# Two divisions and the stores of their rows, moved three slots later on GpSimd and SyncE

## The chip, the core and the metric

The kernel runs on one core of a Trainium2 chip. The core has a matrix engine (TensorE, PE in the profile, with its weight loads as PEld), a vector engine (VectorE, DVE), an activation engine (ScalarE, ACT), a general engine (GpSimd, POOL) and SyncE (SP), which here only issues transfers. Each engine works through its own list of instructions in order, and an instruction that waits holds up all that stand behind it on that engine. Transfers between memory (HBM) and the on-chip buffers go through 16 DMA engines. They are issued either by SyncE (the hardware queue q1) or by GpSimd (the software queue q0). The metric is the time of one execution in device microseconds, as a median of runs.

## The reference

What is computed is a linear attention followed by a two-layer network. With `phi(x) = [exp(p), exp(-p)]`, where `p = x @ w_phi` less the largest absolute value of its row:

```
q_p, k_p = phi(q), phi(k)                 # 8 batches x 8 heads x 576 rows, 64 -> 2 x 128 features
kv  = k_p^T @ v;   z = sum of k_p over rows
x   = (q_p @ kv) / (q_p . z + 1e-6)       # 4608 tokens x 512
h   = x @ w_in                            # 512 -> 2048
g   = max(h, 0) + alpha * min(h, 0)
out = g @ w_out                           # 2048 -> 512
```

## The kernel before, in words

The attention goes through 32 pairs of heads, one after the other, interleaved in a software pipeline. For pair `i` the numerator (128 rows of two heads by 576 tokens) is copied to a tile `s`, and the denominators are inverted by DVE, written to a small array `rec_d` in memory, and read back spread over the partitions into a tile `rr` (`spread`, line 533, two transfers). GpSimd then multiplies `rr = s * rr` (`finish`, line 538), which is the division of the reference, and SyncE writes the tile to `x_d` in memory (`store`, line 541).

Behind the attention comes the network. Its first block of 512 tokens is computed plainly: for each of 16 slices of the hidden layer PE computes `h` (`up2`, lines 584 to 586), ACT and DVE make `r`, `g`, `gh` and `gl` of it (lines 261, 265, 142, 152), and PE adds the slice to four output banks (`down2`, lines 594 to 596). The weights of this block are loaded by SyncE (`load_up` 663, `load_down` 651) as buffers come free. The other eight blocks go two at a time through a scheme with seven products instead of eight, which needs sums and differences of weight blocks. These sums are made once, beside the first block, by `sums` (line 697): GpSimd loads four blocks of a weight (`su<-a_d` or `sv<-a_d`, line 713), DVE makes four sums in place (lines 720, 721, 726, 727), ACT halves two results into a high part (line 146), DVE makes the low part (line 149), and GpSimd stores both results (`us_d<-su`, `vs_d<-sv`, line 741). The results lie in four buffers, which other tiles of decoded weights use too, so that an ACT half must wait until the store of the buffer's last tenant is complete.

Everything around the change stands in one list `todo` of pairs (time, action), sorted by time. The attention's entries come from `places(i)`, with one unit of time for one pair; from 33.05 on the list belongs to the network. In that later part the written order binds PE, SyncE and GpSimd alone. DVE and ACT are put in order by a scheduler, which places an instruction by when it computes its inputs to be ready. The rows of the last two pairs, 30 and 31, lie in the last 576 token columns of `x_d`, which only the last pair of token blocks reads (`prepare(4)`), near the end of the run.

The lines that matter: `places` gives the times `x` (of `finish`) and `xs` (of `store`); `end` is true for pairs 30 and 31; `SUMT` and `SUMS` set the times of the weight sums.

Of the kernel before, what the change touches and what calls it, by code (L numbers as in the profile page):

```python
# [60 lines left out]
def places(i):  # L61
    early = True
    end = i >= NPAIR - 2
    lag = 0 if i >= NPAIR - 4 else 1
    first = {}
    if i == 0:
        first = dict(
            kz=0.5093, ka=0.6934, ko=0.8124, kr=1.1197, kc=1.4241,
            n=1.8361, q=(0.96, 0.9362, 0.4904), qe=(0.9994, 1.0, 0.8939),
        )  # L70
    if i == 1:
        first = dict(kz=0.0015, ka=0.0046, ko=0.0058)
    return dict(
        ld=-2.1 if i > 2 else -1.9,
        lv=-0.17 if i > 2 else -0.45,
        p=(-0.9955 if early else -0.997, -0.2197),
        pl=-0.219 if i > 2 else -0.2217,
        ke=(0.005, 0.008) if i > 2 else (-0.1643, -0.0202),
        kz=1.0035,
        ka=1.0012,  # L80
        ko=1.0045,
        kr=1.0191,
        kc=1.1461,
        q=(1.4089, 1.4543, 1.3558),
        qe=(1.4364, 1.4627, 1.3892),
        d=2.004,
        ds=2.0047,
        n=2.0062,
        s=2.1311,
        d9=2.025,  # L90
        dv=lag + 2.7686 if early else 2.842 if end else 2.7432,
        rd=lag + 2.82,
        rr=lag + 3.03 if lag else 3.06,
        x=lag + 3.72,
        xs=lag + 4.05 if lag else 3.851,
        y=0.0055,
        s0=2.007,
    ) | first
# [26 lines left out]
def fused_kernel(ctx: ExitStack, tc: tile.TileContext, kq, v, w_phi, w_in, w_out, alpha, out):  # L125
# [178 lines left out]
    def attention_units(i):  # L304
# [235 lines left out]
        def store():  # L540
            nc.sync.dma_start(x_d[hp, :, b * S : (b + 1) * S], c["r"])

        at = places(i)
        us = [
            (at["ld"], load),
# [599 lines left out]
```

## Time and profile before

| | us |
|---|---|
| median of 3 runs | 1003.82 (1002.67 to 1003.88) |
| profiled execution, whole | 1001.65 |
| profiled execution, span | 999.9 |
| PE busy | 976.2 |
| DVE busy | 744.1 |
| ACT busy | 625.5 |
| POOL busy | 242.2 |

The span is the time from the first to the last instruction in the trace of one profiled execution; the whole time lies 1.75 us above it. Times in the rows are microseconds from the start of the span. The attention ends at about 323 us, and the first block of the network, with the weight sums beside it, runs until about 407 us. The stretch that the change touches begins there.

### The profile page before, as it was taken

How to read it: one execution, taken by the hardware profiler on the slowest of the kernel's cores; microseconds unless marked ns; L12 is line 12 of the kernel's file. 1: busy time of each engine (PE TensorE's matmuls, PEld its weight loads, DVE VectorE, ACT ScalarE, POOL GpSimd, SP SyncE). 2: the span in 40 equal slices, each digit the busy share in tenths (PEclk: the TensorE clock that was granted, in tenths of full speed). 3: DMA queues.
4: the chain of work that ended last, by engine and by line, in shares of the span. 5: the costliest groups of instructions: out<-in, count | busy, mean ns of one | idle time of the engine just before them, and what ended most of it. 6: DMA issues, size and time to landing. Idle time of an engine off the chain costs nothing.

```text
span 999.9 us, 19129 instructions
## 1 busy us (share of the span) xinstructions
PE 976.2 (98%) x7200; PEld 789.5 (79%) x7200; DVE 744.1 (74%) x1174; ACT 625.5 (63%) x1224; POOL 242.2 (24%) x218
## 2 busy tenths in 40 slices
PE   8999999999999999899999999999999999999998
PEld 7666666666666877787888888888888888888887
DVE  6888888888885577687997465888366977565874
ACT  4799899899898234455566454665455655554553
POOL 1466676666665131121000000000000000000001
PEclk9999999999999999999999999999999999999999
DMA  5588889999885999996767566768567677565565
GB/s 180 186 297 289 301 300 310 313 316 328 310 278 195 333 352 417 378 330 215 275 215 276 183 238 204 273 209 275 202 208 250 234 238 265 169 221 192 185 221 182
DMA packets 99339, 258.52 MB, mean 259 GB/s; under 512 B 12656, under 2 KB 13296, under 8 KB 99248
## 3 DMA queue, kind: packets, MB, share of 16 engines
q1 hardware_dynamic: 88816, 221.71, 65.5%
q0 software_dynamic: 10000, 35.39, 9.2%
q8 instruction: 57, 0.93, 0.4%
q14 instruction: 34, 0.28, 0.1%
q10 hardware_dynamic: 432, 0.20, 0.1%
HBM read 196.16 MB, written 60.96 MB: 257 GB/s over the span
## 4 chain that ended last, share of the span: by engine, by line
PE 58%; DMA 9%; DVE 3%; issue 3%; ACT 1%; POOL 1%; SPq 0%; ACTq 0%; DVEq 0%; POOLq 0%
PE pa L876 5%; PE pa L878 5%; PE pa L877 5%; PE qa L878 5%; PE qa L877 5%; PE qa L876 5%; PE pc L876 3%; PE pc L877 3%; PE pc L878 3%; DMA xr<-x_d 2%; DMA sv<-a_d 2%; PE qc L878 2%; DMA vs_d<-sv 2%; PE qc L877 2%; PE qc L876 2%
## 5 line engine op out<-in xcount | busy, mean ns | idle before, releaser
L142 ACT CAST hv<-g 128x512 fp32r<-128x512 f32 x224 | 135.4, 618 | 80.8 <-PE qa L878 44.3
L152 DVE TENSOR_TENSOR hv<-g,hv 128x512 fp32r<-128x512 f32 x224 | 150.3, 685 | 40.4 <-ACT hv L142 39.1
L766 POOL DMA_DIRECT2D out_dram<-pt x35 | 19.0, 543 | 503.3 <-ACT pt L1044 419.0
L354 DVE TENSOR_REDUCE m<-pj 128x8 f32<-128x1024 f32 (+2 forms) x67 | 78.5, 1172 | 36.1 <-PE pj L350 36.1
L878 PE MATMUL qa<-hv,wv 128*128 128x512 f32 (+1 forms) x257 | 97.3, 379 | 0.1
L877 PE MATMUL qa<-hv,wv 128*128 128x512 f32 (+1 forms) x257 | 97.2, 378 | 0.0
L876 PE MATMUL qa<-hv,wv 128*128 128x512 f32 (+1 forms) x257 | 97.2, 378 | 0.0
L355 DVE TENSOR_TENSOR t<-pj,m 128x1024 f32<-128x1024 f32 (+2 forms) x67 | 78.8, 1177 | 4.4
L350 PE MATMUL pj<-w_sb,raw 64*128 64x128 f32 x1024 | 75.3, 287 | 4.1 <-DVE t L355 4.1
L350 PEld LDWEIGHTS pj<-w_sb,raw 64*128 64x128 f32 x1024 | 63.2, 189 | 19.5 <-issue 15.3
L377 POOL TENSOR_TENSOR y<-xk 128x1024 f32<-128x1024 f32 x30 | 71.0, 2368 | 5.2 <-ACT xk L369 5.2
L488 PE MATMUL n<-qf,sf 128*64 128x288 f32 x512 | 69.2, 412 | 0.0
L204 POOL TENSOR_TENSOR aw<-cw,aw 128x512 int32<-128x512 int32 x32 | 41.7, 1302 | 110.6 <-DVE aw L200 92.0
L369 ACT ACTIVATE xk<-t 128x1024 f32<-128x1024 f32 (+1 forms) x66 | 64.1, 1022 | 5.0 <-DVE t L355 5.0
L896 ACT ACTIVATE r<-g 128x512 f32<-128x512 f32 x65 | 37.4, 622 | 46.9 <-DVE g L892 46.8
L390 PE MATMUL kv<-xk,v 128*64 128x256 f32 x512 | 62.3, 385 | 0.0
L477 ACT ACTIVATE qf<-qt 128x512 f32<-128x512 f32 x116 | 60.8, 648 | 0.0
L142 ACT CAST xo<-xr 128x512 fp32r<-128x512 f32 x56 | 33.6, 619 | 43.4 <-DVE xr L819 21.9
L897 DVE SCALAR_TENSOR_TENSOR g<-r,al,g 128x512 f32<-128x512 f32 x65 | 45.9, 747 | 17.1 <-ACT r L896 16.9
L878 PEld LDWEIGHTS qa<-hv,wv 128*128 128x128 f32 x257 | 48.6, 189 | 7.3 <-DVE hv L152 0.5
L152 DVE TENSOR_TENSOR xo<-xr,xo 128x512 fp32r<-128x512 f32 x56 | 38.7, 701 | 20.8 <-ACT xo L142 20.4
L876 PEld LDWEIGHTS qa<-hv,wv 128*128 128x128 f32 x257 | 48.6, 189 | 6.9
(203 smaller groups left out, 2534.3 us busy)
## 6 DMA issues: line engine op xcount, KB each, us to landing
wv<-vs_d SPq DMA_DIRECT2D x64, 512.0 KB, 4.3
ws<-us_d SPq DMA_DIRECT2D x54, 512.0 KB, 3.8
wv<-v_d SPq DMA_DIRECT2D x48, 512.0 KB, 5.9
wa<-u_d SPq DMA_DIRECT2D x37, 512.0 KB, 5.5
raw<-kq_dram SPq DMA_DIRECT2D x31, 576.0 KB, 6.7
v<-v_dram SPq DMA_DIRECT2D x32, 320.0 KB, 5.1
rr<-rec_d SPq DMA_DIRECT2D x64, 144.0 KB, 3.8
x_d<-rr SPq DMA_DIRECT2D x32, 288.0 KB, 3.6
```

What stands on the lines that cost most here:

```text
L142: return act.copy(dst, src)
L152: return eng.tensor_tensor(dst, src, f(hi), op=ALU.subtract)
L350: pe.matmul(dst[h, j], lhsT=c["raw"][hs, ts], rhs=w_sb[hs], start=True, stop=True)
L354: dve.tensor_reduce(m, src, axis=AX.X, op=ALU.max, apply_absolute_value=True)
L355: dve.tensor_tensor(t[:, hs, js], src, m.unsqueeze(3).broadcast_to([P, nh, nj, FD]), op=ALU.subtract)
L369: act.activation(x[:, a, :, js], c["t", 0][:, :, js], AF.Exp, scale=sg)
L377: pool.tensor_tensor(y, x[:, :, : 2 * FD], x[:, :, 2 * FD :], op=ALU.add)
L390: pe.matmul(c["kv"][h * D : (h + 1) * D, 0:2], lhsT=c["v"][:, tp, h, :], rhs=c["x", ch][:, :, h, j, :], start=tp == 0, stop=tp == NV - 1,)
L488: pe.matmul(ps[h * D : (h + 1) * D, :], lhsT=c["st"][:, a, h * D : (h + 1) * D], rhs=c["qf"][:, h, a, u * HS : (u + 1) * HS], start=a == 0 ...
L876: pe.matmul(ps, lhsT=wh, rhs=xh, start=first, stop=False, skip_group_check=True)
L877: pe.matmul(ps, lhsT=wl, rhs=xh, start=False, stop=False, skip_group_check=True)
L878: pe.matmul(ps, lhsT=wh, rhs=xl, start=False, stop=end, skip_group_check=True)
```

## The change

For pairs 30 and 31, `finish` gets the time 6.75 and `store` 6.76, where before both had about 3.72 and 3.85. The times of `spread`, and of everything else, stay.

```diff
-        x=lag + 3.72,
-        xs=lag + 4.05 if lag else 3.851,
+        x=lag + 3.72 if not end else 6.75,
+        xs=lag + 4.05 if lag else 6.76 if end else 3.851,
```

On GpSimd, where the weight sums begin, the order before is the following. `rr<-s,rr` is the multiplication of `finish`, once for pair 30 and once for pair 31; `su` and `sv` are the tiles of the weight sums (number 0 the loaded blocks, 1 and 2 the results), and `xr` are rows of `x_d` for the second and third token blocks.

```order
L713 DMA su_0_5210<-a_d 128x1024
L713 DMA sv_0_5212<-a_d 128x1024
L538 TENSOR_TENSOR rr_5216<-s_5024,rr_5216 128x576
L713 DMA su_0_5277<-a_d 128x1024
L741 DMA us_d<-su_1_5264 128x1024
L741 DMA us_d<-su_2_5268 128x1024
L801 DMA xr_1_5330<-x_d 128x1024
L538 TENSOR_TENSOR rr_5294<-s_5158,rr_5294 128x576
L713 DMA sv_0_5346<-a_d 128x1024
L741 DMA vs_d<-sv_1_5337 128x1024
L741 DMA vs_d<-sv_2_5342 128x1024
```

In the changed kernel the same place on GpSimd reads:

```order
L713 DMA su_0_5210<-a_d 128x1024
L713 DMA sv_0_5212<-a_d 128x1024
L713 DMA su_0_5275<-a_d 128x1024
L741 DMA us_d<-su_1_5263 128x1024
L741 DMA us_d<-su_2_5267 128x1024
L801 DMA xr_1_5328<-x_d 128x1024
L713 DMA sv_0_5342<-a_d 128x1024
L741 DMA vs_d<-sv_1_5334 128x1024
L741 DMA vs_d<-sv_2_5339 128x1024
L713 DMA su_0_5416<-a_d 128x1024
L741 DMA us_d<-su_1_5408 128x1024
L741 DMA us_d<-su_2_5413 128x1024
```

The multiplication of pair 30 has moved behind the last row shown, that of pair 31 three transfers further on. On SyncE, likewise, the two stores of line 541 have moved from between the loads of down weights (line 651) to places behind the loads for hidden slices 10 to 13, and the spread of pair 31 (line 533) stands behind two of these loads as it did.

The instructions of DVE are the same ones, but the scheduler has put those of the weight sums, from the fourth sum on, earlier among those of the first block. Here is DVE before, from `g` of hidden slice 6 on.

```order
L265 SCALAR_TENSOR_TENSOR g_0_6_5415<-r_0_6_5396,al_82,h_0_6_5379 128x512
L149 SCALAR_TENSOR_TENSOR su_2_5417<-su_0_5277,su_2_5417 128x2x256
L152 TENSOR_TENSOR gl_0_6_5428<-g_0_6_5415,gh_0_6_5426 128x512
L819 TENSOR_TENSOR xr_0_3099<-xr_0_3099 128x512
L152 TENSOR_TENSOR xo_6_0_5470<-xr_0_3099,xo_6_0_5470 128x512
L265 SCALAR_TENSOR_TENSOR g_0_7_5465<-r_0_7_5449,al_82,h_0_7_5430 128x512
L152 TENSOR_TENSOR gl_0_7_5477<-g_0_7_5465,gh_0_7_5475 128x512
L819 TENSOR_TENSOR xr_0_3099<-xr_0_3099 128x512
L720 TENSOR_TENSOR sv_0_5346<-sv_0_5346 128x256
L721 TENSOR_TENSOR sv_0_5346<-sv_0_5346 128x256
L152 TENSOR_TENSOR xo_1_0_5521<-xr_0_3099,xo_1_0_5521 128x512
L726 TENSOR_TENSOR sv_0_5346<-sv_0_5346 128x256
```

And DVE in the changed kernel, from the same `g` on:

```order
L265 SCALAR_TENSOR_TENSOR g_0_6_5411<-r_0_6_5392,al_82,h_0_6_5375 128x512
L149 SCALAR_TENSOR_TENSOR su_2_5413<-su_0_5275,su_2_5413 128x2x256
L152 TENSOR_TENSOR gl_0_6_5424<-g_0_6_5411,gh_0_6_5422 128x512
L720 TENSOR_TENSOR sv_0_5342<-sv_0_5342 128x256
L819 TENSOR_TENSOR xr_0_3099<-xr_0_3099 128x512
L721 TENSOR_TENSOR sv_0_5342<-sv_0_5342 128x256
L726 TENSOR_TENSOR sv_0_5342<-sv_0_5342 128x256
L152 TENSOR_TENSOR xo_6_0_5466<-xr_0_3099,xo_6_0_5466 128x512
L727 TENSOR_TENSOR sv_0_5342<-sv_0_5342 128x256
L265 SCALAR_TENSOR_TENSOR g_0_7_5461<-r_0_7_5445,al_82,h_0_7_5426 128x512
L152 TENSOR_TENSOR gl_0_7_5473<-g_0_7_5461,gh_0_7_5471 128x512
L819 TENSOR_TENSOR xr_0_3099<-xr_0_3099 128x512
```

The fourth sum (lines 720 to 727 on `sv`) stood behind `gl` of slice 7 and stands behind `gl` of slice 6 now. The later sums move by about half a slice, and ACT's halves with them. PE's order is the same in both kernels.

## Rows read from the trace of the kernel before

**Rows 1.** The page: its span and the share of PE.

```profile
span 999.9 us, 19129 instructions
...
PE 976.2 (98%) x7200; PEld 789.5 (79%) x7200; DVE 744.1 (74%) x1174; ACT 625.5 (63%) x1224; POOL 242.2 (24%) x218
```

**Rows 2.** Waits of PE over the whole run: total, times, longest, in us.

```profile
PE pa L876 <- ACT u L888: 4.3, 2, 2.5
...
PE po L596 <- DVE gl L152: 2.3, 2, 1.2
PE po L594 <- ACT gh L142: 2.2, 3, 1.4
```

**Rows 3.** Stretches: length, busy per engine, granted clock, DMA share, GB/s.

```profile
326.00:328.00 2.00, 2.00 (x11) 1.75 (x10) 0.37 (x1) 0.00 (x0) 0.00 (x0) 1.00 0.63 190
...
338.00:344.00 6.00, 4.55 (x21) 3.34 (x20) 3.71 (x6) 3.37 (x6) 1.02 (x2) 1.00 0.91 272
...
352.00:358.00 6.00, 4.92 (x23) 4.05 (x22) 4.61 (x7) 1.74 (x3) 3.92 (x8) 1.00 0.74 213
360.00:410.00 50.00, 47.45 (x213) 39.42 (x212) 36.34 (x66) 23.43 (x42) 10.09 (x19) 1.00 1.02 411
362.00:366.00 4.00, 3.53 (x16) 2.46 (x15) 3.02 (x6) 2.52 (x5) 0.53 (x1) 1.00 1.03 420
374.00:378.00 4.00, 2.28 (x10) 1.37 (x9) 2.82 (x7) 0.62 (x1) 1.06 (x2) 1.00 1.02 408
...
418.00:422.00 4.00, 1.46 (x8) 0.95 (x7) 4.00 (x9) 2.99 (x6) 0.91 (x2) 1.00 1.00 391
430.00:432.00 2.00, 0.35 (x2) 0.00 (x0) 1.94 (x4) 2.00 (x5) 0.00 (x0) 1.00 0.92 358
450.00:454.00 4.00, 2.11 (x11) 1.52 (x10) 3.70 (x8) 2.60 (x5) 0.53 (x1) 1.00 0.85 300
454.00:458.00 4.00, 4.00 (x12) 3.22 (x11) 3.40 (x7) 0.57 (x1) 0.00 (x0) 0.57 0.28 114
```

**Rows 4.** POOL in order of time: start, length, instruction, idle time before it.

```profile
324.85 0.54 POOL L713 DMA_DIRECT2D sv<-a_d  x1
335.29 1.60 POOL L538 TENSOR_TENSOR rr<-s,rr 128x576 f32<-128x576 f32 x1 [9.90 <-DMA rr<-rec_d]
336.83 0.59 POOL L713 DMA_DIRECT2D su<-a_d  x1
...
350.81 1.41 POOL L538 TENSOR_TENSOR rr<-s,rr 128x576 f32<-128x576 f32 x1 [11.79 <-DMA rr<-rec_d]
352.16 0.60 POOL L713 DMA_DIRECT2D sv<-a_d  x1
...
355.39 0.54 POOL L713 DMA_DIRECT2D sv<-a_d  x1
```

**Rows 5.** The chain that ended last, in order of time, one piece.

```profile
355.39 20.44 DMA sv<-a_d
```

**Rows 6.** DVE in order of time.

```profile
335.64 1.52 DVE L727 TENSOR_TENSOR sv<-sv 128x256 f32<-128x256 f32 x1
...
350.92 1.85 DVE L149 SCALAR_TENSOR_TENSOR su<-su,su 128x512 fp32r<-128x512 f32 x1 [0.40 <-ACT su L146]
...
375.85 0.43 DVE L720 TENSOR_TENSOR sv<-sv 128x256 f32<-128x256 f32 x1 [1.11 <-DMA sv<-a_d]
...
415.05 0.43 DVE L720 TENSOR_TENSOR sv<-sv 128x256 f32<-128x256 f32 x1 [3.55 <-DMA sv<-a_d]
```

**Rows 7.** ACT in order of time.

```profile
338.26 0.63 ACT L146 ACTIVATE sv<-sv 128x512 fp32r<-128x512 f32 x1 [1.94 <-DMA v_d<-raww]
...
362.77 0.63 ACT L146 ACTIVATE sv<-sv 128x512 fp32r<-128x512 f32 x1 [3.63 <-DMA vs_d<-sv]
```

**Rows 8.** SyncE's DMA issues in order of time.

```profile
328.06 0.41 SPq L235 DMA_DIRECT2D v_d<-raww  x1
...
336.91 0.32 SPq L541 DMA_DIRECT2D x_d<-rr  x1
...
352.24 0.32 SPq L541 DMA_DIRECT2D x_d<-rr  x1
```

## The prediction

> **What bounds the kernel now.** I read the page first: PE is busy for 976.2 of 999.9 us [rows 1], so whatever a change gives or costs shows up as PE idle time, and the whole of that is 23.7 us. Second the waits of PE: hardly any is on a transfer directly. The longest are on ACT's copies of `u`, and on `gl` and `gh` of the first block [rows 2]. Third the table by stretches, to see where these waits lie and what the DMA engines do there [rows 3]. The reader is to see two things. PE idles in six places between 338 and 432 us: 1.45 us in 338 to 344 (length less PE busy), 1.08 in 352 to 358, 0.47 in 362 to 366, 1.72 in 374 to 378, 2.54 in 418 to 422, 1.65 in 430 to 432, together 8.91. And from 360 to 410 the DMA share is 1.02 at 411 GB/s, full, while there are holes before it: 0.37 of 2 us at 326, 0.09 of 6 us at 338, 0.26 of 6 us at 352, together 0.74 + 0.54 + 1.56 = 2.84 us in which the transfers could have been at work.
>
> Then GpSimd's own order, which explains the holes [rows 4]. The multiplication of pair 30 stands in front of the third load of the weight sums and waits 9.90 us for its spread row, until 335.29. That of pair 31 stands in front of the fourth load and waits 11.79 us, until 350.81. Behind it a burst goes out at once: from 352.16 to 355.39 two `sv` loads with one `su` load and four stores between them. The last load of the burst takes 20.44 us to be used [rows 5]. DVE gets it at 375.85 [rows 6], and the `gl` that stands behind on DVE is what PE waits for in 374 to 378. The burst's first stores are late as well: ACT waits 3.63 us for one at 362.77 [rows 7], and PE idles in 362 to 366. So the stalls of PE from 352 to 378 go back to GpSimd being held by two divisions that nobody needs soon: their rows are read by the last pair of token blocks alone.
>
> **The change part by part.**
>
> *The two multiplications.* They go from in front of the third and the fourth load to behind the stores of the third and of the fourth sum. Each keeps its 1.41 to 1.60 us on GpSimd [rows 4] and finds its spread row landed there, so the waits of 9.90 and 11.79 us go. GpSimd issues the third load right behind the second, at about 325.4 instead of 336.83, and the fourth about when the first stores are out, near 336.5 instead of 352.16. The second sum's stores no longer stand behind 350.81 but follow DVE's low parts, about 1.5 us behind the ACT half of 338.26 [rows 7]. I count 11 us of lead for these.
>
> *What that gives PE.* The four stalls from 352 to 432 that rows 3 show outside the first (1.08, 0.47, 1.72, and 2.54 with 1.65) have different standing. The first three, 3.27 us, hang directly on the held queue, and I take them as gone. The two after 410 have a sum's load (DVE idle 3.55 us before 415.05 [rows 6]) or store in their way too, but the later loads are issued only when DVE has worked off the sum before. Part of the lead is used up by then: I take half, 2.10 of 4.19. Bounds: nothing of it, or all 4.19.
>
> *What it costs.* The third load and the first two stores now go out ahead of, or beside, the store `v_d<-raw` that SyncE issues at 328.06 [rows 8], and for that store ACT already waits 1.94 us at 338.26 with the first stall of PE behind it. One such transfer is 128 x 1024 x 4 bytes = 0.524 MB, at 411 GB/s [rows 3] 1.28 us. All three in front of the store delay it 3.8 us, none of them 0. The two queues were both at work in those microseconds, so I take the middle, 1.9 us added to the first stall.
>
> Beside the rows on the full stretch stands a rule of the Trainium skill, "DMA: Bandwidth & Descriptors", section "Issuing engines are not separate DMA queues": transfers of all engines run on the same 16 DMA engines, and issuing them from several at once saves the issue time alone. By that rule the lead is worth at most the 2.84 us of the holes, and nothing where it only takes from SyncE's loads (the first rival). With its share of 1.02 the trace agrees from 360 on.
>
> *DVE.* While the multiplication of pair 30 ran, a DVE sum took 1.52 us where the same size takes 0.43, and beside that of pair 31 a low part took 1.85 us [rows 6]. Such collisions move with the multiplications to other DVE work, some 15 and 8 us later. I count them as 0: at worst one of them falls on a `gl` that PE waits for, 1.1 us, and at best both fall on slack, -1.1.
>
> The rule on this is in the Trainium skill, "SBUF — State Buffer", section "Who interferes with whom": the port pair that DVE and GpSimd share is an exclusive lock, held for a whole instruction. The trace fits that, since 1.52 less 0.43 is near the 1.60 us of the multiplication less a head start. By the rule the price is up to 1.6 us for each collision wherever it falls, in place of my 0.
>
> *SyncE's queue.* The first store of `x_d` goes out at 336.91 and the second at 352.24 [rows 8], each right after its multiplication, and down weights stand behind both. Without them these loads go out when PE frees their buffers. No wait of PE on them is among the longest [rows 2], so that counts 0. The stores themselves, two of 0.29 MB, merely move. Their readers come hundreds of microseconds later.
>
> *Sum.* -3.27 - 2.10 + 1.9 = -3.5 us. The holes are a check from another side: if the stretch from 360 on is bound by transfers alone, its end moves by 2.84 us. I take the value between them, 3.2 us. Against the profiled execution that is 1001.65 - 3.2 = 998.4; the median of the runs lies 2.17 us above that execution, so the time forecast is 1003.82 - 3.2 = 1000.6.
>
> **The rivals.**
>
> *The transfers are the bound, and the lead is worth nothing.* For it speaks the share of 1.02 over 50 us [rows 3]: loads that start earlier take their share from the weight loads of SyncE, which then come later, and the first stall grows by the 1.9 us above. Of the 2.84 us some 0.9 are left: 1003. Against it speaks that PE waits for sums and not for weights.
>
> *Slower: DVE meets the sums too early.* The scheduler has put the fourth sum behind `gl` of slice 6 instead of slice 7, the later ones about half a slice earlier. DVE is done with slice 6 around 353 (350.92 + 1.85 [rows 6]), with the load issued near 336.5: room for 16.5 us. The point from which this decides is there: a load that takes the 20.44 us of rows 5 is 3.9 us late, and `g`, `gh`, `gl` of slice 7 stand behind it on DVE. With nothing gained elsewhere that is 1003.8 + 3.9 = 1007.7. For it: the DMA engines are full. Against: those 20.44 us come from the burst, which the change spreads out.
>
> *All of it goes.* If the whole chain of sums runs ahead, the stalls after 410 go too, and with DVE in another order also the 1.89 us in 450 to 454 and the half clock behind them (granted 0.57 over 4 us, mostly the lower of the levels 1.2 and 2.4 GHz: 4 x 0.43 = 1.72 us) [rows 3]. That is 3.27 + 4.19 + 1.89 + 1.72 = 11.1 less the 1.9: 994.6. Against it: in 450 to 454 DVE is busy for 3.70 of 4 us, and its amount of work is not touched.
>
> **How the numbers follow.** Chances: forecast 0.48 (own range 998 to 1002.5), transfers as the bound 0.23, sums too early 0.18, all of it 0.11. A measurement of this kernel tells about 0.2%, 2 us, from no change. Faster by more than that: most of the forecast, 0.44, and all of the last, together 0.55. Within it: 0.04 of the forecast, 0.22 of the second, together 0.26. Slower: 0.18 and 0.01, together 0.19. The range of 995.5 to 1005.5 leaves out the better half of "sums too early" at one end and most of "all of it" at the other.
>
> **What would show it.** In the changed profile GpSimd should issue three loads in a row before 326 us and a fourth near 337, both multiplications should stand after 350 with no wait on `rr<-rec_d`, and the DMA share of 352 to 358 should be near 1. PE's stalls at 352, 362 and 374 should be gone or under 0.5 us each, the first one should be 2 to 4 us, and no `sv<-a_d` should take 20 us. The forecast is wrong if PE waits in the first block for `g` or `gl` behind a DVE that waits for `sv<-a_d`, or if a weight load (`wd`, `wa`, `ws`) turns up among PE's waits, or if what is gained by 410 is lost again by 460.

## The result and the profile after

The changed kernel takes **993.22 us** (median of 4 runs, 991.36 to 993.86), the kernel before 1003.85 us beside it: a ratio of **0.9887 [0.9862, 0.9911]**, 10.6 us faster. I had forecast 1000.6, so the direction was right and the size was a third of what came. The profiled execution of the changed kernel took 991.36 us, 10.3 less than that of before.

The page of the changed kernel, span and engines (answers to [rows 1]):

```profile
span 989.6 us, 19136 instructions
...
PE 971.8 (98%) x7200; PEld 788.8 (80%) x7200; DVE 742.8 (75%) x1174; ACT 625.6 (63%) x1224; POOL 242.2 (24%) x218
```

GpSimd in the changed kernel, in order of time (answers to [rows 4]). Three loads go out in a row, the fourth follows at 337.57, and neither multiplication waits for its row:

```profile
324.00 0.71 POOL L713 DMA_DIRECT2D su<-a_d  x1 [4.77 <-PE n L488]
324.71 0.54 POOL L713 DMA_DIRECT2D sv<-a_d  x1
325.24 0.53 POOL L713 DMA_DIRECT2D su<-a_d  x1
...
337.57 0.53 POOL L713 DMA_DIRECT2D sv<-a_d  x1
...
350.40 1.43 POOL L538 TENSOR_TENSOR rr<-s,rr 128x576 f32<-128x576 f32 x1
351.76 0.60 POOL L713 DMA_DIRECT2D sv<-a_d  x1
...
359.15 1.44 POOL L538 TENSOR_TENSOR rr<-s,rr 128x576 f32<-128x576 f32 x1
```

The stretches of [rows 3] in the changed kernel, with one more, 378 to 398:

```profile
326.00:328.00 2.00, 2.00 (x11) 1.76 (x10) 0.00 (x0) 0.00 (x0) 0.00 (x0) 1.00 0.98 322
338.00:344.00 6.00, 3.66 (x16) 2.59 (x15) 3.30 (x5) 3.06 (x6) 1.70 (x4) 1.00 1.02 408
352.00:358.00 6.00, 6.00 (x29) 5.25 (x29) 5.28 (x11) 3.48 (x7) 0.35 (x1) 1.00 1.02 410
362.00:366.00 4.00, 4.00 (x20) 3.52 (x19) 3.60 (x8) 2.26 (x4) 0.70 (x2) 1.00 1.03 414
374.00:378.00 4.00, 4.00 (x21) 3.49 (x20) 3.05 (x6) 0.68 (x2) 0.00 (x0) 1.00 1.02 413
378.00:398.00 20.00, 17.93 (x84) 15.38 (x83) 15.84 (x28) 9.99 (x18) 2.13 (x4) 1.00 1.03 417
418.00:422.00 4.00, 4.00 (x20) 3.51 (x19) 3.90 (x10) 2.28 (x4) 0.12 (x1) 1.00 0.87 287
430.00:432.00 2.00, 2.00 (x11) 1.76 (x10) 1.97 (x5) 1.98 (x5) 0.98 (x2) 1.00 0.51 178
450.00:454.00 4.00, 3.68 (x18) 2.87 (x16) 4.00 (x9) 3.29 (x7) 0.31 (x1) 1.00 0.66 202
454.00:458.00 4.00, 3.29 (x15) 2.92 (x16) 4.00 (x8) 1.61 (x4) 1.88 (x5) 1.00 0.60 239
```

The holes in the transfers are filled: 322, 408 and 410 GB/s where [rows 3] have 190, 272 and 213. Of the six stalls of PE five are gone, the two behind 410 with them, and so is the half clock at 454. The first stall has grown from 1.45 to 2.34 us, and between 378 and 398 there is a new one of 2.07. Waits of PE over the whole run in the changed kernel (answers to [rows 2]: total, times, longest) name them both:

```profile
PE po L594 <- ACT gh L142: 2.3, 1, 2.3
PE pa L876 <- DMA wa<-u_d: 2.1, 1, 2.1
```

Where the time went is read best between three marks on PE: the first matmul into the output banks of the first block, the last one there, and the first that reads `wv` in a later block. For the kernel before, with the columns of [rows 3], these stretches are:

```profile
323.75:406.05 82.30, 77.33 (x349) 64.96 (x348) 55.86 (x98) 31.61 (x57) 18.08 (x30) 1.00 0.98 372
406.05:482.65 76.60, 70.33 (x315) 59.93 (x313) 60.52 (x105) 42.83 (x78) 13.85 (x26) 0.98 0.85 309
```

and the same work in the changed kernel:

```profile
323.60:403.82 80.22, 75.81 (x350) 65.45 (x348) 55.73 (x101) 33.02 (x60) 18.43 (x31) 1.00 1.02 395
403.82:472.95 69.13, 68.10 (x314) 58.75 (x313) 58.84 (x104) 41.38 (x76) 13.26 (x25) 1.00 0.86 321
```

The first block is 2.08 us shorter, the stretch behind it 7.47, and what follows 0.60. So between these two executions the transfers differ most before 358 us, and the time mostly after 406. What may lie between are the weight sums. In the kernel before, DVE and ACT wait for their loads and for the stores that free their buffers (324 to 480 us; total, times, longest):

```profile
DVE sv L720 <- DMA sv<-a_d: 8.2, 5, 3.5
...
ACT sv L146 <- DMA vs_d<-sv: 12.8, 6, 3.6
```

In the changed kernel the first of these is

```profile
DVE sv L720 <- DMA sv<-a_d: 1.6, 2, 0.9
```

and the second does not occur. The sum whose load DVE awaited for 3.55 us at 415.05 [rows 6] starts at 411.32 without a wait:

```profile
411.32 0.41 DVE L720 TENSOR_TENSOR sv<-sv 128x256 f32<-128x256 f32 x1
```

Not every wait of this kind fell: DVE's waits for `su<-a_d` were 5.0 us before and are 7.3 now.

### The profile page after: what moved, and what is told of

The parts are those of the page before. It is cut to its first block, busy times and chain, and to the rows that moved or that the text cites. A ratio compares the mean times of both kernels' runs of the same rounds, so it can differ in the third digit from the quotient of the medians.

```text
span 989.6 us, 19136 instructions
## 1 busy us (share of the span) xinstructions
PE 971.8 (98%) x7200; PEld 788.8 (80%) x7200; DVE 742.8 (75%) x1174; ACT 625.6 (63%) x1224; POOL 242.2 (24%) x218
## 4 chain that ended last, share of the span: by engine, by line
PE 66%; DMA 4%; DVE 3%; issue 1%; ACT 0%; SPq 0%; ACTq 0%; DVEq 0%
PE pa L876 5%; PE pa L877 5%; PE pa L878 5%; PE qa L877 5%; PE qa L878 5%; PE qa L876 5%; PE pc L877 3%; PE pc L878 3%; PE pc L876 3%; PE qc L878 3%; PE qc L877 2%; PE qc L876 2%; DMA wa<-u_d 1%; PE kv L390 1%; PE qb L876 1%; PE qb L877 1%
## 5 line engine op out<-in xcount | busy, mean ns | idle before, releaser
L877 PEld LDWEIGHTS qa<-hv,wv 128*128 128x128 f32 x257 | 48.6, 189 | 6.9
L878 PEld LDWEIGHTS qa<-hv,wv 128*128 128x128 f32 x257 | 48.6, 189 | 6.9
L876 PEld LDWEIGHTS qa<-hv,wv 128*128 128x128 f32 x257 | 48.6, 189 | 6.8
```

Source lines behind the costliest of these rows:

```text
L876: pe.matmul(ps, lhsT=wh, rhs=xh, start=first, stop=False, skip_group_check=True)
L877: pe.matmul(ps, lhsT=wl, rhs=xh, start=False, stop=False, skip_group_check=True)
L878: pe.matmul(ps, lhsT=wh, rhs=xl, start=False, stop=end, skip_group_check=True)
```

## The experiments

Beside the theory of the prediction (A: GpSimd was held by the two divisions, so the loads and stores of the sums came late) there were two others. B: both queues, GpSimd's and SyncE's, stood behind the same two rows at once, and freeing either fills the hole. C: the scheduler's other order of DVE and ACT, with the sums about half a slice earlier, makes the gain.

**e1: only the stores on SyncE moved.** The divisions stay in GpSimd's way.

```diff
-        xs=lag + 4.05 if lag else 3.851,
+        xs=lag + 4.05 if lag else 6.76 if end else 3.851,
```

> Only the two stores of x_d move three slots later on SyncE; both divisions stay where they were on GpSimd. The scheduler's order on DVE and ACT comes out close to that of the changed kernel, with the weight sums about half a slice earlier. Theory A (GpSimd held by the divisions, so that the loads and stores of the weight sums go out late): no gain, 1002 to 1006 us, GpSimd still idle about 10 and 12 us before the two multiplications, and DVE, which meets the sums earlier, waits longer for their loads. Theory B (SyncE's stores hold up the weight loads of the first block): most of the gain, 993 to 996 us. Theory C (the new order on DVE and ACT makes the gain): 993 to 997 us, with the stalls of PE after 410 us gone.

993.5, ratio 0.9924 [0.9898, 0.9949], with GpSimd still waiting 9.93 and 7.84 us. The divisions in GpSimd's way are then not enough for the loss, which speaks against A and against the prediction's "counts 0" for SyncE; the order of DVE and ACT had changed too, so e7 repeats this run with the order held.

**e2 and e3: one pair moved, on both queues** (`x` and `xs` late for `i == NPAIR - 2`, or for `i == NPAIR - 1`, alone).

> Division and store of pair 30 alone move; pair 31 stays in front of the fourth load. Theory A: the first hold (9.9 us) goes and the third load goes out near 325 us, but GpSimd still waits for the row of pair 31, and the second sum's stores, the fourth load and the burst behind it stay late: a third of the gain or less, 1000 to 1003 us. Theories B and C: near half of the gain, 997 to 1000 us.

995.5, ratio 0.993 [0.991, 0.9949].

> Division and store of pair 31 alone move; pair 30 still holds GpSimd until its row lands near 335 us, in front of the third load. Theory A: the second hold of 11.8 us goes, the stores of the second sum and the fourth load are no longer bunched near 352 us, so most of the gain comes, 993 to 997 us, with the first stall of PE near 1.5 us as before. If the two holds count alike: 998 to 999 us.

991.89, ratio 0.9899 [0.9863, 0.9935]. Either half brings most of the whole by its median, and the two together would be 1.71% where the whole is 1.13%.

**e4: the places of before, without the wait.** The rows of pairs 30 and 31 are spread from the finished denominators of pairs 28 and 29 and issued earlier, so the last two pairs are divided by other pairs' denominators.

```diff
-        rr=lag + 3.03 if lag else 3.06,
+        rr=lag + 3.03 if lag else 2.9 if i == NPAIR - 2 else 2.0 if end else 3.06,
...
-                    c["r"][h * D : (h + 1) * D], rec_d[i : i + 1, h * S : (h + 1) * S].broadcast_to([D, S])
+                    c["r"][h * D : (h + 1) * D], rec_d[i - 2 * (i >= NPAIR - 2) : i + 1 - 2 * (i >= NPAIR - 2), h * S : (h + 1) * S].broadcast_to([D, S])
```

> Both divisions and stores stay at their places on GpSimd and SyncE, but the spread rows of pairs 30 and 31 are read from the denominators of pairs 28 and 29, which are in memory long before, and are issued ahead of the first block's loads: the last two pairs are divided by the wrong denominators. This takes away the wait and leaves the place. Theory A: the gain is there without any move, 992 to 996 us, with no idle time of GpSimd before the multiplications. If the place itself counted (1.4 us of GpSimd each, or the store on SyncE): 1000 us or more.

993.88, ratio 0.9915 [0.9887, 0.9943]. GpSimd waits 2.03 us for the first row and nothing for the second. That speaks for the waiting as the cost, and against the place. But in all four kernels the scheduler had also put DVE and ACT in another order, so C was still open.

**e5, e6, e7: the order of DVE and ACT held.** A list gives, for each of the two engines, the order that another kernel has there, and each instruction gets a scheduling edge (no wait) to the one before it:

```diff
+    for e, rows in ROWS.items():
...
+        for a, b in zip(rows, rows[1:]):
+            tc.add_manual_dep(
+                done[b],
+                done[a].name,
+                mybir.DependencyInfo(mybir.DependencyClass.NoSync, mybir.DependencyReason.DATA),
...
```

> GpSimd's and SyncE's order as in the kernel before (both divisions and the stores of their rows in their old places), but the instructions of DVE and ACT from the first weight sum on are held in the order that they have in the changed kernel. Theory B (both transfer queues stood behind the divisions, and freeing either fills the hole at 352 to 358) expects the time of before, about 1003, with GpSimd's long wait near 350 and the DMA share of 352 to 358 near 0.74 as before. Theory C (the gain comes from DVE's and ACT's new order, in which the weight sums stand about half a slice earlier) expects the changed kernel's time, 993 to 994, with the queues still held. If both are wanted together it lies between, 996 to 1000.

1000.24, ratio 0.9954 [0.9938, 0.9971]. This is less than the time of before, which B alone expects, and far from the changed kernel's time, which C expects. GpSimd and PE in e5:

```profile
351.09 1.41 POOL L538 TENSOR_TENSOR rr<-s,rr 128x576 f32<-128x576 f32 x1 [12.13 <-DMA rr<-rec_d]
```

```profile
PE po L594 <- ACT gh L142: 6.8, 2, 5.2
```

Between the marks used above, the first block of e5 is 4.97 us longer than that of before, and the stretch behind it 7.47 us shorter, as short as in the changed kernel:

```profile
323.98:411.25 87.27, 80.44 (x350) 68.71 (x349) 56.82 (x101) 32.80 (x60) 18.39 (x31) 0.94 0.96 362
411.25:480.38 69.13, 68.10 (x315) 58.75 (x314) 58.84 (x104) 41.42 (x76) 13.26 (x25) 1.00 0.89 321
```

> GpSimd's and SyncE's order as in the changed kernel (divisions and stores late), but DVE's and ACT's instructions held in the order of the kernel before. Theory B expects the changed kernel's time, 993 to 994, with the DMA share of 352 to 358 near 1. Theory C expects about 1003, with PE's stalls at 352 to 378 and 418 to 432 back although no queue is held. Both wanted together: 996 to 1000.

994.92, ratio 0.9905 [0.9885, 0.9925]: with the order of before the freed queues bring 9.9 us of the whole. C is a smaller, second effect.

> Only the stores of the two rows moved to their late places on SyncE, the divisions left where they held GpSimd before, and DVE's and ACT's instructions held in the order of the kernel before. The same edit with the order left to the scheduler gave 993.5. Theory B expects 993 to 996 (SyncE's queue alone fills the hole). Theory C expects about 1003. My first theory, that the held GpSimd is what costs, expects 1003 too, so this one tells only together with the two others: time of before here and time of after with after's queues would bring it back.

995.09, ratio 0.9906 [0.9886, 0.9926]. GpSimd in e7, and the 40 us from 326 to 366:

```profile
336.16 1.52 POOL L538 TENSOR_TENSOR rr<-s,rr 128x576 f32<-128x576 f32 x1 [10.14 <-DMA rr<-rec_d]
...
346.66 1.66 POOL L538 TENSOR_TENSOR rr<-s,rr 128x576 f32<-128x576 f32 x1 [6.86 <-DMA rr<-rec_d]
```

```profile
326.00:366.00 40.00, 37.68 (x166) 32.04 (x165) 26.03 (x44) 13.84 (x24) 10.94 (x18) 0.96 1.00 389
```

SyncE freed alone, GpSimd held for 17 us, order of before: the same gain as both freed, and 389 GB/s where the changed kernel has 390 and the kernel before 335. One thing differs besides: the row of pair 31 lands sooner, so GpSimd's second hold ends at 346.66 where in the kernel before it ends at 350.81.

**e10 and e11: GpSimd free, SyncE held.** The divisions and stores are late, the order of DVE and ACT that of before, and at the stores' old places (in e11 at that of pair 31 alone) SyncE gets a store of 2 x 8 numbers that waits for the spread row.

```diff
+        def hold():
+            nc.sync.dma_start(h_d[i - NPAIR + 2], c["r"][D - 1 : D + 1, :8])
```

> GpSimd free, SyncE held: the changed kernel's late divisions and late stores, DVE and ACT in the order of before, and at the two old places of the stores on SyncE a store of 2 x 8 numbers of the spread row to a spare tensor, which waits for that row alone and so holds the queue until it has landed (about 335 and 350 in before). Only these two tiny stores tell it from the kernel that gave 994.9. Theory S (it is SyncE's queue that was held, with the down weights and the next slices' weights behind the store) expects 1000 to 1004, a DMA share of 352 to 358 near 0.75 and PE's stalls at 352 to 378 back, although GpSimd waits for nothing. Theory G (GpSimd's queue, as I predicted) and theory B (either queue freed is enough) expect 993 to 996.

993.32, ratio 0.9902 [0.9866, 0.9939]. SyncE in e10, and the same 40 us:

```profile
335.54 0.25 SPq L542 DMA_DIRECT2D h_d<-rr  x1
...
349.91 0.25 SPq L542 DMA_DIRECT2D h_d<-rr  x1
```

```profile
326.00:366.00 40.00, 38.23 (x176) 32.84 (x175) 26.98 (x49) 14.50 (x25) 10.32 (x16) 1.00 1.02 391
352.00:358.00 6.00, 6.00 (x30) 5.25 (x29) 4.58 (x9) 2.85 (x5) 0.00 (x0) 1.00 1.03 419
```

That SyncE alone is the cause falls too: held to 349.91 it costs nothing that can be told. GpSimd issued loads and stores up to 340.77 meanwhile, and again from 348.19.

> The same with the tiny store of the last pair alone, so SyncE is held once, at about 342 to 350. Theory S says where the loss sits: if in the second hold, which leaves the hole at 352 to 358, this is nearly as slow as with both, 999 to 1003; if in the first, 994 to 996. Theories G and B expect 993 to 996.

993.48, ratio 0.9902 [0.9869, 0.9935], as e10. Its profiled execution took 2031.38 us, so no row of it is shown.

**e13: both held, without the stores' bytes.** Everything as in the kernel before, but the small store of e10, which here waits for the division, stands in for the large one, which comes late.

> Both queues held as in the kernel before, without the traffic: DVE, ACT and GpSimd in the order of before with both divisions in their old places, and on SyncE at the old places of the stores a store of 2 x 8 numbers of the finished row, which waits for the division just as the store of 0.29 MB did; the whole stores go out late as in the changed kernel. Theory B (the loss is there when both queues are held at once, and either one freed brings the gain) expects 1001 to 1005. If it was the two stores' bytes in front of the loads, or the order alone, it expects 993 to 996.

1003.33, ratio 1.0005 [0.9987, 1.0024]. This is the time of before: what costs is the waiting, not the bytes of the stores. In e13 the 40 us have 325 GB/s, and the hole before 358 is there:

```profile
326.00:366.00 40.00, 38.88 (x179) 33.16 (x178) 26.60 (x45) 14.16 (x25) 10.66 (x17) 1.00 0.95 325
352.00:358.00 6.00, 6.00 (x29) 5.00 (x28) 4.09 (x8) 2.72 (x5) 2.92 (x6) 1.00 0.87 234
```

The place where the time goes is not that of before. In this execution, the shortest of e13's twelve at 998.05 us, the first block takes 85.47 us (82.30 before), and the stretch behind it 70.74 (76.60 before), no longer than with a queue freed (70.95 in e7, 71.01 in e10):

```profile
323.87:409.34 85.47, 78.80 (x349) 66.07 (x348) 58.28 (x102) 33.71 (x61) 19.52 (x33) 0.98 0.99 367
409.34:480.08 70.74, 68.07 (x314) 58.85 (x313) 58.85 (x103) 42.20 (x75) 12.22 (x23) 1.00 0.87 318
```

**e16: GpSimd free, SyncE held for longer.** As e10, with a second small transfer that waits for the first.

> GpSimd free, SyncE held for longer: as the run with the tiny stores that gave 993.3, with a second tiny transfer behind each, which waits for the first to have landed. In that run SyncE was let go at 335.8 and 350.3, 1.4 and 2.4 us sooner than in before (337.3 and 352.7); this takes that difference away, with 337 to 338 and 352 to 353 expected. Theory B expects 993 to 996 still. If those 2 us of SyncE's hold were what brought the gain there, 1000 to 1004.

1004.78, ratio 1.0027 [1.0008, 1.0046], which fits no expectation as written, since the hold went far past its aim. SyncE in e16, and the transfers:

```profile
341.63 0.53 SPq L544 DMA_DIRECT2D h_d<-h_d  x1
...
361.25 0.50 SPq L544 DMA_DIRECT2D h_d<-h_d  x1
```

```profile
326.00:366.00 40.00, 35.21 (x153) 29.59 (x152) 24.16 (x43) 13.27 (x23) 7.40 (x13) 0.96 0.92 316
362.00:366.00 4.00, 4.00 (x20) 3.51 (x19) 2.59 (x5) 2.79 (x5) 0.53 (x1) 1.00 0.68 61
```

Until 341.63 and 361.25, 5 and 10 us longer than in e13: GpSimd's transfers ran out, and the hole is now at 362 to 366, at 61 GB/s. Here PE waits for the weights themselves:

```profile
PE h L590 <- DMA wa<-u_d: 5.2, 4, 1.8
```

GpSimd itself issues nothing from 355.02 to 364.97. So a free GpSimd covers a held SyncE only for as long as its own transfers last. A hold of just the length of before with GpSimd free was not hit: e10 was let go 1.0 and 1.3 us sooner than e13, and e16 later. Those 2.3 us can then be a part of what tells e10 from e13, by an estimate about a third: between them 66 x 40 / 411 = 6.4 us of full transfers are missing (391 and 325 GB/s).

**e18 and e19: one pair moved, order of before held** (the edits of e2 and e3 with e6's list).

> Pair 30 alone moved on both queues (the edit that gave 995.5 with the scheduler's order), with DVE and ACT in the order of before. Both queues are then held once, by pair 31, until about 350. Theory B with the hole before 358 as the cause (both queues held at once, the transfers idle meanwhile) expects 1000 to 1004 if the hold by pair 31 is the one that counts. If the other order of DVE and ACT was not what made 995.5, and it takes both holds to lose, 994 to 997.

1000.76, ratio 0.9968 [0.9947, 0.9989].

> Pair 31 alone moved on both queues, with DVE and ACT in the order of before. Both queues are held once, by pair 30, until about 335. Theory B expects little loss here, since the hole of before at that place is 0.74 to 1.28 us: 993 to 997. If every hold of both queues costs alike, 998 to 1001.

997.6, ratio 0.9939 [0.9915, 0.9963]. The same 40 us in e18 and in e19:

```profile
326.00:366.00 40.00, 37.72 (x167) 32.46 (x167) 27.07 (x45) 13.97 (x25) 9.73 (x16) 0.96 0.96 352
```

```profile
326.00:366.00 40.00, 38.03 (x173) 32.05 (x172) 26.23 (x46) 14.40 (x25) 10.36 (x17) 1.00 0.97 367
```

With the order out of it the parts add up within their intervals: 0.32% and 0.61% against 0.95% for both (e6). By the medians, more than half of the 0.70% of e2 was its other order.

The kernels with the order of before that have a row, by what the transfers moved from 326 to 366 in the profiled execution. The last two columns are of all runs; the ratio is against the kernel before, run beside each:

| kernel | queues held | GB/s | profiled us | median us | ratio |
|---|---|---|---|---|---|
| e10 | SyncE to 349.9 | 391 | 993.66 | 993.32 | 0.9902 |
| e7 | GpSimd to 346.7 | 389 | 994.76 | 995.09 | 0.9906 |
| e6 | none | 383 | 994.92 | 994.92 | 0.9905 |
| e19 | both, by pair 30 | 367 | 997.08 | 997.6 | 0.9939 |
| e18 | both, by pair 31 | 352 | 1000.67 | 1000.76 | 0.9968 |
| before | both, twice | 335 | 1001.65 | 1003.85 | 1 |
| e13 | both, twice | 325 | 998.05 | 1003.33 | 1.0005 |
| e16 | SyncE to 361.3 | 316 | 1003.55 | 1004.78 | 1.0027 |

By the medians the time goes with the bytes, whichever queue is the one held. By the profiled executions, from which the bytes are read, e13 falls out of line. From 391 to 335 GB/s the shortfall is 56 x 40 / 411 = 5.5 us of full transfers; the time is 8.0 us longer by the profiled executions and 10.5 by the medians. So a microsecond missing there costs an estimated 1.5 to 1.9. With other orders of DVE and ACT the same shortfall costs less: e5 has 326 GB/s and 1000.24, e2 338 and 995.5.

**e8, e9, e12, e15, e14: what bounds the changed kernel, and whether something beats it.** e8 stores the last decoded block ahead of the first block's loads (aimed at the first stall), e9 also issues the late `wa` sooner, e15 moves divisions and stores seven slots further (6.75 to 13.75) and nothing else, e12 is e8 with e15. e14 is the changed kernel again, beside e15.

```diff
-        w = W | W0 if blk[:2] == (0, 0) else W | dict(store=0.9) if t > NPAIR - 3 else W
+        w = W | W0 if blk[:2] == (0, 0) else W | dict(low=0.52, store=0.54) if t > NPAIR else W | dict(store=0.9) if t > NPAIR - 3 else W
```

> The changed kernel with the last decode block's low part and its two stores on SyncE written ahead of the first token block's first weight loads. Aimed at the first stall of PE, 2.34 us at 338 to 344, behind ACT's wait of 1.73 us for v_d<-raw. Both theories: that stall falls to 0.5 to 1 us, the weight loads behind come about 1 us later; 991.5 to 993 if nothing is late for it, 993 to 995 if the weight load of 381 (2.07 us wait for wa) takes it back.

992.15, ratio 0.9875 [0.9852, 0.9898]. The first stall falls to 0.17 us, and PE waits 2.5 us for `wa` instead: no gain that can be told.

> A candidate: the changed kernel with the last block's low part and stores early, and the next block's first wa load issued two down weights sooner (about 376 in place of 381), since PE waited 2.07 us for it in the changed kernel. If that wait is one of order on SyncE, 990 to 991; if the transfers are full there (share 1.02 to 1.03), it only changes places with another load, 992 to 993.5.

993.37, ratio 0.99 [0.987, 0.993]. The wait for `wa` only moved.

> A candidate: the changed kernel with the last block's low part and stores early (as in the run that gave 992.15) and the two divisions and their stores seven slots later still, at about 427 to 437, where the DMA share is 0.5 to 0.9 rather than at 355 to 366, where it is 1.02. It takes 0.59 MB, 1.4 us at 411 GB/s, out of the full stretch. If the first block is bound by transfers there now, 1 to 1.4 us better than 992.15, 990.8 to 991.2; if not, 992 to 993.

990.31, ratio 0.9873 [0.9841, 0.9905].

> A candidate: the changed kernel with the divisions and stores seven slots later still (about 427 to 437) and nothing else. If the full stretch of 344 to 410 is what bounds the changed kernel, it gains the 1.4 us of the two stores: 991 to 992 against the changed kernel in this job; if not, no difference within 0.2%.

991.3, ratio 0.9898 [0.9872, 0.9925].

> The changed kernel itself, on the same chip as the others of this job, so that they are compared with it and not with before alone: 992 to 994.5, ratio 0.987 to 0.991.

993.93, ratio 0.9922 [0.9893, 0.995]. e15 lies 2.6 us under it, run beside it, in the direction that 0.59 MB less in the full stretch would give, but the intervals overlap. e12 has the lowest median of all, 990.31; that it beats the changed kernel is not shown.

## Why the prediction was wrong

The step that failed is the worth of the lead behind 410 us: **"Part of the lead is used up by then: I take half, 2.10 of 4.19"**. Between the two profiled executions the stretch behind the first block became 7.47 us shorter, not 2.10. All of the 4.19 went. So did 0.86 of the 1.89 us of idle time between 450 and 458, which the sum left out, and the busy time of PE fell by 2.23 us, for which the sum had no term. How the lead shortens this stretch is not settled: with the order of before it takes 70.30 us in e6, 70.95 in e7 and 71.01 in e10, all with a queue freed, but also 70.74 in e13, and 69.13 in e5 with the other order and both queues held.

The check that stood beside the sum, **"the lead is worth at most the 2.84 us of the holes"**, failed as well. I took the holes from the busy share and not from the GB/s that stand beside it in the same rows. In [rows 3] the three stretches moved 190, 272 and 213 GB/s against 411 when full: (221 x 2 + 139 x 6 + 198 x 6) / 411 = 6.0 us of transfers missing, not 2.84. Nor would 6.0 have been a limit, since 10.3 us came. The check moved the forecast by only 0.3 us, from 3.5 to 3.2. But it agreed with a sum that was too small as well, so that the sum looked confirmed. Of the rule that I drew on (the Trainium skill, "DMA: Bandwidth & Descriptors", section "Issuing engines are not separate DMA queues") the first half agrees with the runs: with either queue held, the other kept the engines at 389 (e7) and 391 GB/s (e10). The second half, that issuing from several engines saves only the time of issuing, leaves out what the runs show: while one queue stood, the other kept the transfers going, and that was worth about 1% of the time (e7 and e10 against e13).

Point by point:

- **The multiplications.** Waits of 9.90 and 11.79 us gone, three loads in a row before 326, the fourth at 337.57: as predicted.
- **The four stalls after the first.** 1.08, 0.47 and 1.72: gone, as predicted. Of 2.54 and 1.65 I took half; all 4.19 went. "Part of the lead is used up by then" was wrong here: the sum at 415.05 came 3.73 us earlier and found its load landed.
- **The first stall.** I added 1.9 us; it grew by 0.89. The mechanism was right, with ACT behind the store `v_d<-raw` in the changed kernel too (1.94 us in [rows 7]):

```profile
339.00 0.63 ACT L146 ACTIVATE sv<-sv 128x512 fp32r<-128x512 f32 x1 [1.73 <-DMA v_d<-raww]
```

- **SyncE's queue "counts 0".** Wrong. Freed alone, with the second hold of GpSimd 4.15 us shorter for it, it brings 0.94% (e7). I asked whether PE waited for the weights behind it; I should have asked whether anything else kept the transfers full while it stood.
- **GpSimd as the cause.** Half right: freeing it was enough (e10), but it was not needed (e7), and while SyncE is free its waiting costs nothing that can be told.
- **DVE's collisions at 0.** The sum beside the first multiplication took 1.08 us at 351.05 where others take 0.42; PE was busy all through 352 to 358, so 0 stands.
- **Not counted:** the stall of 2.07 us for `wa`, which I had named as a sign of being wrong, and on the other side the stretch from 450 to 458 (1.89 us idle before, 0.32 + 0.71 after) and the half clock at 454. Granted 0.57 there before and 1.00 now, it is part of the 2.23 us that PE is busy less behind the first block.

Between the marks that makes, behind the first block, 5.24 us of idle time (6.27 to 1.03) and 2.23 of busy time; in the first block 0.56 of idle and 1.52 of busy time, of which the profile shows no cause, since the number of records (349, 350) and the clock are the same.

Of the rivals, "all of it goes" (994.6, chance 0.11) came nearest: it had the right stalls and the clock. That its number is off by only 1.4 us is partly luck, since it left out the new stall of 2.07 us and the 1.52 us of busy time in the first block, which nearly cancel. "The transfers are the bound" had the right resource and drew the opposite conclusion, that a lead is worth nothing. "DVE meets the sums too early" did not occur in the changed kernel. In e5, where the loads are late, it did in part: the first block is 4.97 us longer there. But the stretch behind it is 7.47 shorter, so that the other order helps, by 0.46% when the queues are held. With them free it is 0.18% between e6 and the changed kernel, which the intervals do not tell from nothing.

Still open: why a microsecond of missing transfers costs more than one, and why the kernel before pays behind the first block and e13, with the same holds and the same order, within it. The waits for `sv<-a_d` and `vs_d<-sv` suggest by what way the loss travels, but no run took that way alone.

## What to carry to other kernels

Here an instruction that waited at the head of a queue cost time only where no other queue's transfers filled the gap. So look at all queues that stand behind the same event, free one, and see in the trace whether its work lasts until the other is let go (it did in e10 and not in e16). Measure a hole in the transfers by bytes, not by busy share. When a change also lets a scheduler reorder other engines, hold their order before splitting the change: without that, e2 and e3 seemed to bring one and a half times the gain between them.

## What was not expected of the hardware

Busy share and throughput came far apart: 0.74 at 213 GB/s [rows 3], and 0.68 at 61 GB/s in e16, where 1.02 goes with 411. And a hold of SyncE that ended at 349.9 us cost nothing that can be told (e10), while one that ended at 361.3 cost the whole gain (e16), as GpSimd's own transfers ran out in between.
